# Group 4's second layer by seven products, three load buffers, and what moves with them

## The chip, the cores and the metric

The kernel runs on one core of a Trainium2 chip. The core has five engines that run their own instruction streams in order: TensorE (PE in the profile, its weight loads PEld), VectorE (DVE), ScalarE (ACT), GpSimd (POOL) and SyncE (SP), which here issues nearly all DMAs. The metric is device time in microseconds, from a median of several executions; less is better.

## The reference

Inputs are q, k and v (8 batches, 8 heads, 576 rows, 64 columns), a layer-norm gain of 512, and two weights of 512 x 2048 and 2048 x 512, all float32. Per head, attention goes by 32 landmarks (means of 18 rows each):

```python
A  = sm(q, k_lm)                 # 576 x 32
Bm = sm(q_lm, k_lm)              # 32 x 32
C  = sm(q_lm, k)                 # 32 x 576
Z  = Bm.T / (norm1(Bm) * norminf(Bm) + 1e-6)
for _ in range(6):
    Z = 2 * Z - Z @ Bm @ Z
x = A @ Z @ C @ v                # heads side by side: 8 x 576 x 512
```

Then a two-layer network with a residual: `x + relu(layer_norm(x) * g @ w1) @ w2`. The output is 8 x 576 x 512 float32.

## The kernel before, in words

**Attention** runs over sets of batches: 0, 1, 2, (3, 4), (5, 6) and 7. For each set, `Coming` holds the parts to come: q, k and v are loaded by SyncE into tiles of 576 KB (`stage`, six buffers), cast to fp16 by GpSimd, turned and summed to landmarks by VectorE, and the landmark sums of a pair are spread by a product `psl` (`spread`). `attention2` then computes scores (`psb`, `psec`, `psea`), the product with v (`pscv`), six iterations (`psn` on TensorE, `st` on VectorE in turn) and finally the rows: each row step is a pair of products `psy`, and VectorE divides into `xblk`, one tile of 128 rows by 512. 4608 rows make 36 blocks, four blocks a group: nine groups, 0 to 8. A group's blocks may come from two batches: batches 3 and 4 end in the middle of block 22, batches 5 and 6 in the middle of block 31.

**The network** is the generator `mlp`, which yields after every one or two matrix products. For each group it takes the normalized and transposed rows `xnT`, computes 16 tiles of the first layer (`psh`, four 128x512 products each, ScalarE's relu writes `hT`), then the second layer. `xnT` comes from four `xn` (one per block, on GpSimd for groups 2 and up) by four DMA transposes on SyncE; the first `psh` of a group waits for all four. `hT` has one buffer.

**Two forms of the second layer.** For groups below `G_FAST` (L45) each block is 16 products of 128x512 into `pso`, and VectorE makes the output tile `ot` from `pso`, the block's deviation factor and `xblk`. Those groups are centered only; the factor `rstd` is applied at the end. From `G_FAST` on, `second_layer` (L870) computes the 512 x 512 result as a 2 x 2 block product with seven half-size products, 16 products of 128x256 each (`psp1`, `psp6`, `psp5` ...), on sums of blocks: `w2_mix` t1 to t4 of the weight (made once, GpSimd) and s1 to s4 of `hT` (made per group, VectorE). Results are added into `xblk`, which is then stored. These groups need `xn` with the factor already in it, so `normalize` (L773) has to run ahead of `center`.

**The order of the work** is written out by hand. Each engine keeps program order. Between the steps of `attention2`, `fill(count)` takes `count` yields out of `mlp`; `steps` (L1150) lists, per set, the count and whether a cast and a turn job of the next set follow. `a_square` runs one waiting statistic per step, `settle` the delayed ones. `block_done` (L746) decides by group what a finished block causes. `center_in_turn` delays a block that is more than one group ahead of `mlp`. `prepare` casts, then issues loads until three are under way.

**Accumulators.** One bank `ps1` (tag `p1`: `psb`, `psse`, `psn`, and batch 7's `psl`), two score tiles of two banks `ps2` (tag `p2`: `psec`, `pscv`, `psea`, `pszc`, `psy`), and three banks `psM` (tag `pm`: `psh`, `pso`, `psp`, earlier `psl`).

In the changed stretch the set (5, 6) goes through its iterations (168 to 185 us) beside group 4's first layer, and through its rows (187 to 206 us) beside group 4's second layer; group 5 follows, beside batch 7.

Of the kernel before, what the change touches and what calls it, by code (L numbers as in the profile page):

```python
# [16 lines left out]
P = 128  # L17
# [3 lines left out]
def kernel(  # L21
# [20 lines left out]
    MCH = HID // P  # L42
    U = H // 4
    NJ = 9
    G_FAST = 5  # L45
    HK, HN = MCH // 2, DM // 2

    scale_qk = 1.0 / (D ** 0.5)
# [30 lines left out]
        keep(nc.tensor.matmul(o, i_, idn, is_transpose=True, tile_position=(0, 0)))  # L79


    def load(src, b, u, queue):
        t = stage.tile([P, 2, NJ, D], FP32, name="stg", tag="stg")
        keep(queue.dma_start(
            out=t[:],
            in_=src[b, 4 * u:4 * u + 4].rearrange("(r e) (t j) d -> (e t) r j d", e=2, j=NJ)))
        return t
# [11 lines left out]

    def load_turned(src, b, u, queue):
        t = stage.tile([P, 2, NJ, D], FP32, name="stg", tag="stg")
        rows = src[b, 4 * u:4 * u + 4].rearrange("(r e) (t j) d -> e t r j d", e=2, j=NJ)
        for half in range(2):
            keep(queue.dma_start(out=t[ts(half, 64), :, :, :], in_=rows[1 - half]))
        return t
# [399 lines left out]

    class Coming:  # L510
        def __init__(self, bs, first_by_pool=0):
            self.bs, self.first_by_pool = bs, first_by_pool
# [29 lines left out]
        def load(self, i, queue=nc.sync):  # L542
            nm, w = self.parts[i]
            b, u = self.units[w]
            src = {"q": q, "k": k, "v": v}[nm]
            self.stg[i] = (load_turned if nm == "v" and u % 2 == 1 else load)(src, b, u, queue)


        def cast(self, i):
# [50 lines left out]

        def spread(self, y):
            part = self.part.pop(y)
            late = self.bs[0] >= 7
            psl = (ps1 if late else psM).tile([P, 2, 8, LM], FP32, name="psl",
                                              tag="p1" if late else "pm")
            for half in range(2):
                MM(psl[:, half, :, :].rearrange("p k c -> p (k c)"),
                   spread16[:, half, :, :, :].rearrange("p e a w -> p (e a w)"),
                   part[:].rearrange("p n w r l x -> p (n w r l x)"))
            lm = asm.tile([P, 8, 2, LM], FP16, name="lm", tag="lm", bufs=3)  # L610
            scalar.copy(lm[:].rearrange("p k h c -> p h k c"), psl[:])
            for i, nm in enumerate(("q", "k")):
                for x in range(2):
                    self.lm[nm, 2 * y + x] = lm[:, ds(4 * i + 2 * x, 2), :, :].rearrange(
                        "p r h (l x) -> p r (h l) x", x=2)
# [130 lines left out]
    def block_done(j):  # L746
        g, u = divmod(j, 4)
        if g >= G_FAST:
            mean_of(j, dve)
            squares.append((at[0] + -4, lambda: normalize(j)))  # L750
            return
# [21 lines left out]
    def normalize(j):  # L773
        g, u = divmod(j, 4)
        square(j)
        if u == 0:
            lnvs[g] = mstat.tile([P, 4], FP32, name="lnv", tag="lnv")
            rstds[g] = mstat.tile([P, 4], FP32, name="rstd", tag="rstd")
        act(lnvs[g][:, u:u + 1], variances[g][:, u:u + 1], AF.Ln, bias=eps_ln[:],
            scale=1.0 / DM)  # L780
        act(rstds[g][:, u:u + 1], lnvs[g][:, u:u + 1], AF.Exp, scale=-0.5)
        center_in_turn(j)
# [72 lines left out]
    w21, w22 = w2_16[:, HK:MCH, 0:HN], w2_16[:, HK:MCH, HN:DM]  # L855

    def mixes_of_w2():
        for i in range(4):
            w2_mix.append(stage.tile([P, HK, HN], FP16, name=f"w2mix{i}", tag="stg"))
        for i in range(2):  # L860
            h_mix.append(stage.tile([P, HK, HN], FP16, name=f"hmix{i}", tag="stg"))
        t1, t2, t3, t4 = [t[:] for t in w2_mix]
        for o, a, b, op in ((t1, w12, w11, ALU.subtract), (t3, w22, w12, ALU.subtract),
                            (t2, t3, w11, ALU.add), (t4, w21, t2, ALU.subtract)):
            for k in range(0, HK, 2):
                pool.tensor_tensor(out=o[:, k:k + 2, :], in0=a[:, k:k + 2, :],
                                   in1=b[:, k:k + 2, :], op=op)
                yield

    def second_layer(g, hT, mixed):  # L870
        t1, t2, t3, t4 = [t[:] for t in w2_mix]
        h11, h12 = hT[:, 0:HK, 0:256], hT[:, HK:MCH, 0:256]
        h21, h22 = hT[:, 0:HK, 256:], hT[:, HK:MCH, 256:]
        s1, s2, s3, s4 = mixed
        x = [x_blk.pop(4 * g + u) for u in range(4)]

        def bank(name):
            return psM.tile([P, 2, HN], FP32, name=name, tag="pm")

        last = g == NGRP - 1  # L880

        def product(to, left, right, first=True, by_k=False):
            order = [(i, k) for i in range(2) for k in range(HK)]
            if by_k:
                order = [(i, k) for k in range(HK) for i in range(2)]
            for n, (i, k) in enumerate(order):
                apart = isinstance(to, list)
                MM(to[i][:] if apart else to[:, i, :], left[:, k, ts(i, P)], right[:, k, :],
                   start=first and (n == 0 or apart and k == 0), stop=k == HK - 1, skip=True)
                if n % 2 == 1 and n < 15:  # L890
                    yield True

        def add(engine, half, col, t, us=(0, 1)):
            for i in us:
                o = x[2 * half + i][:, ts(col, HN)]
                engine.tensor_tensor(out=o, in0=t[i][:] if isinstance(t, list) else t[:, i, :],
                                     in1=o, op=ALU.add)

        pa = bank("psp1")
        yield from product(pa, h11, w11)  # L900
        p1 = mout.tile([P, 2, HN], FP32, name="p1", tag="ot")
        scalar.copy(p1[:], pa[:])
        for half, col in ((0, 1), (1, 1), (1, 0)):
            add(pool, half, col, p1)
        yield True
        pb = bank("psp6")
        yield from product(pb, s2, t2, by_k=True)
        add(dve, 0, 1, pb)
        yield True
        yield from product(pa, h12, w21, False)  # L910
        add(dve, 0, 0, pa)
        if last:
            for u in (0, 1):
                store(4 * g + u, x[u], ts(0, HN))
        for k in range(0, HK, 4):
            dve.tensor_tensor(out=s4[:, k:k + 4, :], in0=h12[:, k:k + 4, :],
                              in1=s2[:, k:k + 4, :], op=ALU.subtract)
        yield True
        yield from product(pb, s3, t3, False)
        add(dve, 1, 1, pb)  # L920
        yield True
        pc = ([psM.tile([P, HN], FP32, name="psp5", tag="pm"),
               ps1.tile([P, HN], FP32, name="psp5", tag="p1")] if last else bank("psp5"))
        yield from product(pc, s1, t1)
        add(dve, 1, 1, pc)
        yield True
        yield from product(pb, h22, t4, False)
        add(dve, 1, 0, pb)
        for u in (2, 3):
            store(4 * g + u, x[u], ts(0, DM), last)  # L930
        yield True
        c = product(pc, s4, w22, False)
        for _ in range(4 if last else 7):
            next(c)
            yield True
        if last:
            add(dve, 0, 1, pc, (0,))
            store(4 * g, x[0], ts(1, HN), True)
        for _ in c:
            yield True  # L940
        add(dve, 0, 1, pc, (1,) if last else (0, 1))
        for u in (1,) if last else (0, 1):
            store(4 * g + u, x[u], ts(1, HN) if last else ts(0, DM), last)
        yield True

    def mix_of_h(hT, mixed, m):
        s1, s2, s3, _ = mixed
        h11, h21, h22 = hT[:, 0:HK, 0:256], hT[:, 0:HK, 256:], hT[:, HK:MCH, 256:]
        k0, k1 = {11: (0, 4), 13: (4, 6), 14: (6, 7), 15: (7, 8)}[m]
        n = ds(k0, k1 - k0)  # L950
        dve.tensor_tensor(out=s1[:, n, :], in0=h21[:, n, :], in1=h22[:, n, :], op=ALU.add)
        dve.tensor_tensor(out=s2[:, n, :], in0=s1[:, n, :], in1=h11[:, n, :], op=ALU.subtract)
        if m == MCH - 1:
            for k in range(0, HK, 4):
                dve.tensor_tensor(out=s3[:, k:k + 4, :], in0=h11[:, k:k + 4, :],
                                  in1=h21[:, k:k + 4, :], op=ALU.subtract)

    def mlp():
        for g in range(NGRP):
# [18 lines left out]
            else:  # L978
# [11 lines left out]
                for m in range(MCH):  # L990
# [6 lines left out]
                    act(hT[:, m, :], psh[:], AF.Relu)  # L997
                    if g >= G_FAST:
                        if m == 0:
                            while not h_mix:  # L1000
                                yield False
                            mixed = [h[:] for h in h_mix] + [hT[:, 0:HK, 256:],
                                                             hT[:, HK:MCH, 0:256]]
                        if m - 1 in (11, 13):
                            mix_of_h(hT, mixed, m - 1)
                        elif m == MCH - 1:
# [142 lines left out]

    steps = [[(10, 1, 0), (12, 1, 1)] + 6 * [(6, 1, 1)] + [(8, 1, 1)] + 5 * [(6, 0, 0)]]  # L1150
    steps += [[(6, 1, 0), (8, 1, 0), (12, 1, 0), (12, 1, 0), (6, 1, 0), (6, 1, 0)] + 4 * [(5, 1, 0)] + [(8, 0, 0)] + 3 * [(6, 0, 0)] + 7 * [(7, 1, 1)]]
    steps += [[(12, 1, 0), (14, 1, 1), (16, 1, 1), (16, 1, 1)] + 6 * [(9, 1, 1)] + [(10, 1, 1)] + 10 * [(8, 1, 1)]]
    steps += [[(15, 0, 0), (18, 0, 0)] + 6 * [(12, 0, 0)] + [(12, 0, 0)] + 5 * [(12, 0, 0)]]
    mixing = mixes_of_w2()
    for c, after, plan in zip(sets, sets[1:] + [None], steps):
# [3 lines left out]
        for n, ((count, casts, jobs), _) in enumerate(zip(plan, attention2(c.bs, c))):  # L1159
# [4 lines left out]
            a_square()  # L1164
            if after:
                prepare(after, casts, jobs)
            if c in sets[2:] and not sets[-1].casts:
                for _ in range(1):
                    next(mixing, None)
    settle()  # L1170
# [36 lines left out]
```

## Time and profile before

| | |
|---|---|
| median of 6 executions | 320.16 us (316.34 to 321.72) |
| profiled execution | 318.57 us |
| its span, first to last instruction | 316.8 us |
| granted TensorE clock | 1.000 |
| busy: TensorE / VectorE / ScalarE / GpSimd | 304.3 / 181.6 / 160.9 / 161.2 us |
| stretch 168 to 186 us: TensorE / VectorE / GpSimd busy | 17.33 / 8.09 / 13.48 us |
| stretch 186 to 202 us: TensorE / VectorE / GpSimd busy | 16.00 / 10.72 / 11.22 us |
| stretch 219 to 233 us: TensorE / VectorE / GpSimd busy | 14.00 / 8.82 / 7.39 us |

The span runs from the first to the last instruction of the profiled execution, and that execution's own time is 1.8 us longer. Busy times of different engines overlap. The stretches are those of group 4's first layer, group 4's second layer (classical form) and group 5's second layer (seven products). Matrix products overlap in the pipeline, so a product's mean duration in a list is longer than the pace; the pace is a stretch's time divided by its products. Times inside a stretch are given in us from the start of the span.

### The profile page before, as it was taken

The page shows a single profiled execution, that of the slowest core. Times are in us where ns is not written, and L with a number is a line of the kernel's source. Part 1 is how long each engine was busy: PE and PEld are TensorE (multiplying, and loading weights), DVE is VectorE, ACT ScalarE, POOL GpSimd, SP SyncE. Part 2 cuts the span into 40 slices and gives each one's busy share as a digit, 9 for nine tenths or more (in the row PEclk, how much of TensorE's full clock was granted, in tenths as well). Part 3 has the DMA queues.
Part 4 walks back from the last instruction along what each step waited for, and adds up shares of the span by engine and source line. Part 5 has one row for each costly group of instructions (what it writes and reads, how often), then busy time and mean ns, then how long its engine had stood idle before and what let it go on. Part 6 is the DMA issues. An engine that isn't in the chain of part 4 may idle for free.

```text
span 316.8 us, 8388 instructions
## 1 busy us (share of the span) xinstructions
PE 304.3 (96%) x3424; PEld 173.9 (55%) x3424; DVE 181.6 (57%) x487; ACT 160.9 (51%) x329; POOL 161.2 (51%) x218
## 2 busy tenths in 40 slices
PE   8889999999997989999999999999999999999994
PEld 8558754443443534544454444445854784685583
DVE  3667239868793325899376337746634860561372
ACT  2476853479225861267536646776038706505600
POOL 4489878908997695583003939900900360040050
PEclk9999999999999999999999999999999999999999
DMA  7999999769999995580087004330054016005013
GB/s 276 391 386 384 385 388 267 252 150 366 212 246 193 381 266 129 98 251 19 6 226 167 0 2 95 70 71 0 3 118 83 0 35 151 18 0 132 2 25 110
DMA packets 38862, 50.35 MB, mean 159 GB/s; under 512 B 17572, under 2 KB 18088, under 8 KB 38824
## 3 DMA queue, kind: packets, MB, share of 16 engines
q1 hardware_dynamic: 38504, 49.43, 54.9%
q8 instruction: 27, 0.44, 0.6%
q10 hardware_dynamic: 320, 0.39, 0.4%
q14 instruction: 11, 0.09, 0.1%
HBM read 36.70 MB, written 9.44 MB: 146 GB/s over the span
## 4 chain that ended last, share of the span: by engine, by line
PE 83%; DVE 9%; DMA 4%; issue 1%; ACT 1%; POOL 1%; SPq 0%; DVEq 0%; POOLq 0%
PE psh L75 40%; PE psp L75 16%; PE pso L75 15%; PE psy L75 3%; DVE part L69 2%; DMA stg<-in_k_dram 2%; DVE xblk L69 2%; PE psn L75 2%; PE pscv L75 2%; DMA xnT<-xn 1%; DVE ot L69 1%; PE psec L75 1%; DVE xT L69 1%; POOL natv L69 1%; PE psea L75 1%
## 5 line engine op out<-in xcount | busy, mean ns | idle before, releaser
L75 PE MATMUL psh<-xnT,w 128*128 128x512 f16 (+1 forms) x640 | 135.3, 359 | 1.3 <-DMA xnT<-xn 1.3
L69 ACT ACTIVATE hT<-psh 128x512 f16<-128x512 f32 x144 | 84.2, 598 | 78.3 <-PE psh L75 77.8
L75 PEld LDWEIGHTS <-w 128*128 128x128 f16 x640 | 58.7, 98 | 58.3 <-issue 4.6
L75 PEld LDWEIGHTS <-hT 128*128 128x128 f16 x640 | 60.9, 98 | 35.2 <-issue 1.5
L75 PE MATMUL pso<-w,hT 128*128 128x512 f16 x320 | 76.6, 380 | 0.0
L69 POOL TENSOR_TENSOR xblk<-p,xblk 128x256 f32<-128x256 f32 x24 | 17.4, 762 | 62.4 <-ACT p L69 62.4
L69 POOL CAST nat<-stg 128x1152 f16<-128x1152 f32 x28 | 31.6, 1145 | 16.0 <-DMA stg<-in_q_dram 14.4
L69 ACT ACTIVATE junk<-xblk,negm 128x512 f16<-128x512 f32 x36 | 25.9, 719 | 21.4 <-POOL negm L69 13.8
L69 POOL TENSOR_SCALAR xn<-xblk,negm,rstd 128x512 f16<-128x512 f32 x16 | 13.5, 856 | 43.8 <-ACT rstd L69 34.6
L69 DVE SCALAR_TENSOR_TENSOR xblk<-psy,rcpd 128x512 f32<-128x512 f32 (+1 forms) x40 | 27.6, 691 | 1.8
L69 DVE SCALAR_TENSOR_TENSOR st<-st,psn 128x128 f16<-128x128 f16 (+2 forms) x36 | 11.4, 316 | 28.0 <-PE psn L75 28.0
L69 DVE TENSOR_TENSOR xblk<-psp,xblk 128x256 f32<-128x256 f32 x48 | 18.2, 418 | 16.1 <-PE psp L75 15.9
L75 PE MATMUL psp<-w,hT 128*128 128x256 f16 x192 | 23.4, 273 | 0.0
L69 POOL CAST natv<-stg 128x1152 f16<-128x1152 f32 x16 | 18.3, 1161 | 7.2 <-DMA stg<-in_v_dram 7.2
L69 DVE TENSOR_TENSOR hmix<-hT 128x256 f16<-128x256 f16 (+2 forms) x16 | 6.8, 424 | 25.6 <-ACT hT L69 25.5
L69 DVE STREAM_TRANSPOSE xT<-nat 128x576 uint32<-128x576 uint32 x24 | 18.5, 769 | 0.0
L69 DVE TENSOR_REDUCE part<-xT 128x32 f16<-128x576 f16 x26 | 18.3, 745 | 0.1
L69 DVE SCALAR_TENSOR_TENSOR ot<-pso,rstd,xblk 128x512 f32<-128x512 f32 x20 | 14.9, 747 | 5.1 <-PE pso L75 5.0
L69 DVE RECIPROCAL rcpd<-psy 128x8 f32<-128x8 f32 (+1 forms) x40 | 8.1, 203 | 16.3 <-PE psy L75 15.7
L75 PE MATMUL psy<-zcbd,ea 128*128 128x260 f16 (+1 forms) x80 | 15.6, 277 | 0.7 <-DVE zcbd L69 0.5
L75 PE MATMUL psp<-w2mix,hT 128*128 128x256 f16 x128 | 15.5, 273 | 0.0
L75 PE MATMUL psp<-w2mix,hmix 128*128 128x256 f16 x128 | 15.3, 273 | 0.0
(116 smaller groups left out, 328.6 us busy)
## 6 DMA issues: line engine op xcount, KB each, us to landing
stg<-in_q_dram SPq DMA_DIRECT2D x16, 576.0 KB, 7.9
stg<-in_k_dram SPq DMA_DIRECT2D x16, 576.0 KB, 7.1
wstg<-in_moe_w_ch_dram SPq DMA_DIRECT2D x16, 512.0 KB, 6.9
stg<-in_v_dram SPq DMA_DIRECT2D x10, 576.0 KB, 10.5
out_dram<-ot SPq DMA_DIRECT2D x40, 128.0 KB, 2.7
stg<-in_v_dram SPq DMA_DIRECT2D x12, 288.0 KB, 11.5
out_dram<-xblk SPq DMA_DIRECT2D x26, 128.0 KB, 2.3
xnT<-xn SPq DMA_TRANSPOSE x28, 2.5
```

Source lines behind the costliest of these rows:

```text
L69: return lambda *args, **kw: keep(getattr(self.engine, op)(*args, **kw))
L75: keep(nc.tensor.matmul(o, l, r, start=start, stop=stop, tile_position=(rb, cb), skip_group_check=(skip or cb != 0)))
```

## The change

`G_FAST` becomes 4, so group 4's second layer also goes by seven products. The mixes of `w2` are therefore needed earlier and beside live load buffers: `t1` is made in place in the weight (`last_mix_of_w2`, four VectorE sums under group 4's first layer), the other three take three of the six buffers of `stage`, and the loads of batches 5 to 7 go through a ring of three. Group 4 keeps `s1` in two output tiles and makes `s2` in place of `h11` after the first product (`mix_less`); its seven products stand in another order, and one of them takes the bank `ps1`. Groups 4, 5 to 8 are normalized four blocks at a time (`normalize`), and group 4's means go to GpSimd. The spreads of the sets from batch 5 on take a score tile (`ps2`) instead of `psM` or `ps1`. The counts of the set (5, 6) become 7 in the iterations (9 before) and 10 in the rows (8 before). The mixing starts in set (3, 4) at step 16.

```diff
-    G_FAST = 5
+    G_FAST = 4
...
+            t = None
+            if self.bs[0] >= 5:
+                if len(ring) < 3:
+                    ring.append(stage.tile([P, 2, NJ, D], FP32, name="ring", tag="stg"))
+                    ring_at[0] = len(ring) - 1
+                t = ring[ring_at[0]]
+                ring_at[0] = (ring_at[0] + 1) % 3
...
-            late = self.bs[0] >= 7
-            psl = (ps1 if late else psM).tile([P, 2, 8, LM], FP32, name="psl",
-                                              tag="p1" if late else "pm")
+            late = self.bs[0] >= 5
+            psl = (ps2 if late else psM).tile([P, 2, 8, LM], FP32, name="psl",
+                                              tag="p2" if late else "pm")
...
         if g >= G_FAST:
+            if g in (4,):
+                later.append(lambda: mean_of(j, pool))
+                squares.append((at[0], lambda: normalize(j)))
+                return
...
         square(j)
+        if g not in (3,):
+            if u == 3:
+                deviations(g)
+                for i in range(j - 3, j + 1):
+                    center_in_turn(i)
+            return
...
+    def last_mix_of_w2(k):
+        dve.tensor_tensor(out=w12[:, k:k + 2, :], in0=w12[:, k:k + 2, :],
+                           in1=w11[:, k:k + 2, :], op=ALU.subtract)
...
+        def mix_less(o, a):
+            n = HK // len(a)
+            for k in range(0, HK, 4):
+                dve.tensor_tensor(out=o[:, k:k + 4, :], in0=a[k // n][:, ds(k % n, 4), :],
+                                  in1=o[:, k:k + 4, :], op=ALU.subtract)
+
+        def mix(o, a, b):
+            for k in range(0, HK, 4):
+                dve.tensor_tensor(out=o[:, k:k + 4, :], in0=a[:, k:k + 4, :],
+                                  in1=b[:, k:k + 4, :], op=ALU.subtract)
+
+        def by_way_of_sbuf(bank_, name, where):
+            t = mout.tile([P, 2, HN], FP32, name=name, tag="ot")
+            scalar.copy(t[:], bank_[:])
+            for half, col in where:
+                add(pool, half, col, t)
+
+        def p1_done(pa):
+            by_way_of_sbuf(pa, "p1", ((0, 1), (1, 1), (1, 0)))
+
+        def p2_done(pa):
+            add(dve, 0, 0, pa)
...
+            mix(s4, h12, s2[0])
...
         pa = bank("psp1")
         yield from product(pa, h11, w11)
+        p1_done(pa)
+        if not apart:
+            mix_less(h11, s1)
...
+        pc = bank("psp5")
         yield from product(pc, s1, t1)
         add(dve, 1, 1, pc)
         yield True
+        yield from product(pa, h12, w21, False)
+        p2_done(pa)
+        yield True
+        pb = bank("psp6")
+        yield from product(pb, s2, t2)
+        add(dve, 0, 1, pb)
+        yield True
+        pd = (bank("psp4") if g in (3,) else
+              ps1.tile([P, 2, HN], FP32, name="psp4", tag="p1"))
+        yield from product(pd, h22, t4)
+        by_way_of_sbuf(pd, "p4", ((1, 0),))
+        yield True
+        yield from product(pc, s4, w22, False)
+        add(dve, 0, 1, pc)
+        for u in (0, 1):
+            store(4 * g + u, x[u], ts(0, DM))
+        yield True
+        yield from product(pb, s3, t3, False)
+        by_way_of_sbuf(pb, "p7", ((1, 0), (1, 1)))
...
+                                mixed = [[mout.tile([P, HK // 2, HN], FP16, name="s1", tag="ot")[:]
+                                          for _ in range(2)], []]
...
+                        if g == G_FAST and m in (2, 4, 6, 8):
+                            last_mix_of_w2(m - 2)
...
-    steps += [[(12, 1, 0), (14, 1, 1), (16, 1, 1), (16, 1, 1)] + 6 * [(9, 1, 1)] + [(10, 1, 1)] + 10 * [(8, 1, 1)]]
+    steps += [[(12, 1, 0), (14, 1, 1), (16, 1, 1), (16, 1, 1)] + 6 * [(7, 1, 1)] + [(10, 1, 1)] + 10 * [(10, 1, 1)]]
...
-            if c in sets[2:] and not sets[-1].casts:
+            if (c.bs[0], n) >= (3, 16):
```

## The prediction

> **What bounds the kernel now.** I read the busy shares first, then the slices, the chain that ended last, TensorE's waits, and then the stretches of the engines around the change.
>
> ```profile
> PE 304.3 (96%) x3424; PEld 173.9 (55%) x3424; DVE 181.6 (57%) x487; ACT 160.9 (51%) x329; POOL 161.2 (51%) x218
> ...
> PE   8889999999997989999999999999999999999994
> ...
> PEclk9999999999999999999999999999999999999999
> ```
>
> TensorE is busy in 96% of the span at a full clock; no other engine passes 57%. Only less TensorE work, or a new TensorE stall, moves the end. The chain in order of time gives the price of both forms of a layer, because the last groups run there undisturbed:
>
> ```profile
> 197.78 1.73 PE pso L75 x8
> ...
> 274.09 12.23 PE psp L75 x112
> 286.31 13.81 PE psh L75 x64
> 300.13 12.25 PE psp L75 x112
> ```
>
> A 128x512 product takes 13.81/64 = 0.216 us (so do the `pso` of group 4's second layer: 1.73/8), a 128x256 one of the seven-product form 12.25/112 = 0.109 us. TensorE's own waits add up to 7.6 us, most of them in the first 120 us; one lies in the changed stretch, at 180.56:
>
> ```profile
> PE psn L75 <- ACT lm L69: 0.7, 1, 0.7
> ```
>
> There an iteration product `psn` waited until ScalarE had emptied the spread `psl`, which stood in the same single bank.
>
> **What the change takes away.** (a) Group 4's second layer: 64 x 0.216 = 13.8 us becomes 112 x 0.109 = 12.25 us: -1.56 us, between -1.5 and -1.6 by the rows. (b) Batch 7's spread goes to a score bank, so the 0.7 us above ends: -0.7 (0 if VectorE is late there anyway). Nothing else on TensorE goes: its order keeps all other products. So -2.26 us is the most there is, 0.7% of the time.
>
> **What it adds, edit by edit.**
>
> Three load buffers: a load is now issued only when the cast three loads earlier is done. The loads of batches 5 to 7 used to be issued in a bunch (six within 100.25 to 104.2). Now the load that takes the buffer of the cast of 105.23 goes out when that cast ends, at 106.4, and with 4.9 us to land (issue 100.25, cast released at 105.2) it is there at 111.3; the one after the cast that ends at 110.5 at 115.4. GpSimd wants them at 111.56 and 115.72 (its casts of before). Margins of 0.3 to 0.5 us, and behind them GpSimd idles 3.25 us before 125.39: cost 0, at most some 1 to 3 us if loads come later and that cover is used up. Behind a waiting load on SyncE's queue stand only further loads and stores there.
>
> The mixes of w2: GpSimd makes twelve pieces of 1.15 us in place of sixteen, between 135 and 181 instead of 178 to 206, beside its casts. First used at about 191: cost 0 on TensorE. Their four missing pieces become four VectorE sums in `w12`, 0.42 us each by the 128x512 `hmix` rows.
>
> Centering by groups of four: group 4's four `xn` can start only after its deviations (ScalarE, about 157.2 in place of 136.5). The first is done at 158.0, the fourth transpose goes out 3.9 us later and lands 2.5 us after that (rows under (d)): 164.4; the first layer begins at 168.07, slack 3.6 us. Behind them on GpSimd stand batch 7's casts (160.3 instead of 139.2); VectorE's transpose of the first (160.58) starts 0.8 us late, and `psn` uses that stretch at 169.7. Group 7: after the row that completes block 31 TensorE has 28 x 0.216 + 112 x 0.109 + 8 x 0.11 = 19 us of work, the chain to its input takes about 12. Cost 0; 1 to 2 us if such slack is used up.
>
> Spreads in the score bank: two buffers, last read over 1 us before each spread: 0. Rows further apart: the same row products; cost 0 as long as VectorE keeps up.
>
> (c) **VectorE in the iterations.** Between 168 and 182 the steps have 7 products in place of 9, and VectorE gets the four sums in `w12`. In VectorE's sums of two SBUF operands a wait shows. First GpSimd's timeline, then VectorE's at the same time (start, us, engine, operation, out<-in):
>
> ```profile
> 139.15 3.32 POOL L69 CAST nat<-stg 128x1152 f16<-128x1152 f32 x3
> ```
> ```profile
> 140.18 1.24 DVE L69 TENSOR_TENSOR part<-sT 128x64 f16<-128x64 f16 x1
> ...
> 143.37 0.39 DVE L69 TENSOR_TENSOR part<-sT 128x64 f16<-128x64 f16 x1
> ```
>
> The same operation takes 1.24 or 0.39 us: it ends when GpSimd's current instruction ends (the second cast, at 141.4). GpSimd will be busy without a break from 157 to 181, so each of the five such sums ahead of the fifth iteration may wait up to 1.15 us. Laid out with rows (0.42 + two reduces of 0.66 + 0.35 in one step; 0.42 + 0.70 + 0.20 + 0.25 in the next two) VectorE is 1.2 us ahead of `psn` without waits and up to 3.7 us behind with all of them. The eleven rows of `part<-sT` have a mean of 0.49 against 0.19 alone, a wait of 0.3: five of them less the lead of 1.2 give 0.3. As GpSimd never pauses here I take +0.5 us; bounds 0 and 3.7.
>
> (d) **Group 5's input.** This is the term that I expect to matter. Before, groups 5 and later were centered block by block. Now block 23 completes under group 4's first product, the four `xn` stand on GpSimd behind six `xblk` additions of that product, and group 5 begins as soon as the seventh product ends. Rows for each link:
>
> ```profile
> 221.65 4.18 POOL L69 TENSOR_TENSOR xblk<-p,xblk 128x256 f32<-128x256 f32 x6 [15.19 <-ACT p L69]
> 225.82 3.22 POOL L69 TENSOR_SCALAR xn<-xblk,negm,rstd 128x512 f16<-128x512 f32 x3
> ```
> ```profile
> 220.13 1.29 DVE L69 TENSOR_TENSOR hT<-hT 128x1024 f16<-128x1024 f16 x2
> ...
> 225.49 1.49 DVE L69 TENSOR_TENSOR hT<-hT,hmix 128x1024 f16<-128x1024 f16 x2
> ```
> ```profile
> 220.98 0.58 ACT L69 COPY p<-psp 128x512 f32<-128x512 f32 x1 [1.42 <-PE psp L75]
> ```
> ```profile
> 264.14 5.16 SPq L807 DMA_TRANSPOSE xnT<-xn  x4
> ```
> ```profile
> xnT<-xn SPq DMA_TRANSPOSE x28, 2.5
> ```
>
> From the end of the first product: copy 0.7 (product end to GpSimd's start), six additions 4.2, one `xn` 0.77, last of four transposes issued 3.9 later (5.16 less one issue of 1.2), 2.5 to land, 0.1: 12.15 us. TensorE has meanwhile six products and five row pairs: 96 x 0.109 + 5 x 0.225 = 11.6 us (0.225: what a `psy` pair takes between products at 195.45). So 0.5 us is missing even undisturbed. And the three `xn` above took 3.22 us where 3 x 0.75 = 2.25 is usual: they stood behind VectorE's pair of `hT` sums at 225.49. Group 4's form has two such pairs (`mix_less`, and the fourth mix), both inside this chain: 12.15 + 2 x 0.95 - 11.6 = +2.4 us. Bounds: 0.5 without any meeting, 3.6 if each pair also waits for half an addition. Behind the stall on TensorE stands everything.
>
> The Trainium skill, page "SBUF — State Buffer", section "Who interferes with whom", says that a VectorE instruction with two SBUF inputs and a GpSimd instruction that reads SBUF exclude each other for a whole instruction, whichever started first. The 1.24 us and the 3.22 us rows agree with it. By that rule both pairs of (d) count and the sum stays at +0.6; without any exclusion (d) would be 0.5 us, (c) 0, and the sum -1.8 us. The page "TensorE: Matmul & The Clock Gate", section "HAM oscillation — how this bites in real kernels", speaks against the change: gaps over about 3.4 us halve the clock for a while, so a stall of (d)'s upper bound could cost some 1.7 us more by that page; no gap here is longer than 1.3 us, and the clock row shows no drop.
>
> **Sum.** -1.56 - 0.7 + 0.5 + 2.4 = +0.6 us. The profiled execution took 318.57 us, its span 316.8 us; the span would become 317.4, that execution 319.2. The six runs have their median at 320.16, 1.6 us above the profiled one; on that scale the forecast is 320.8 us. About 1% (3.2 us) is what a measurement of this kernel can tell from no change, so this is none.
>
> **Rivals.**
> 1. The stalls do not come: the pairs miss GpSimd's work, or a late VectorE delays the second layer so that the input is there in time. Then -2.26 + 0.5, 318.4 us. For it: (d) undisturbed misses by 0.5 us only. Against: the pair at 225.49 met GpSimd exactly so.
> 2. Slower: two-input sums on VectorE behind GpSimd's instructions, in both places. It has some 16 us of work in the 17 us from the last iteration to the end of group 4's second layer (zcbd 1.35, sums for the mixes 5.5, six rows at 1.1, additions 2.7), so the waits have no room. Price: (c) at 3.7 and (d) at 3.6: -2.26 + 7.3 = +5.0, 325.2 us. It decides from 5.5 us of stalls on, where the loss passes 1%. For it: GpSimd has no gap from 157 to 181. Against: `part<-sT` waits 0.3 us on the mean, far less than a whole instruction.
> 3. Three buffers starve the casts: 1 to 3 us more than the forecast, 322 us. Against: the margins above and the idle 3.25 us.
>
> **Chances.** Forecast 0.5 (its own range 318.8 to 322.8), rival 1 0.2, rival 2 0.25, rival 3 0.05. Faster by over 1% would need 316.9, under the most that TensorE can give: 0.04 for what I overlook. Slower by over 1%, from 323.4 on: rival 2 and a little of the forecast's tail, 0.28. Within 1%: 0.68. The range goes from rival 1 less 0.8 to rival 2: 317.6 to 325.2.
>
> **What would show it.** (a) 112 `psp` in group 4, 0.109 us each. (b) No `psn` waiting for `lm`. (c) `psn` or `psl` waiting for VectorE's `st` or `part` between 173 and 182. (d) `psh` waiting about 2.4 us for a transpose near 199 us, the largest wait of the second half. Buffers: no new GpSimd wait for a load. The forecast is wrong if that `psh` wait is absent, or if TensorE waits for VectorE inside group 4's products.

## The result, and the profile after

The median is 321.25 us for the changed kernel (34 executions, 318.67 to 325.86) and 319.25 us for the kernel before on the same chips (71 executions). The ratio is 1.0077, with a 95% interval of 1.0059 to 1.0096: about 2.5 us slower (1.9 to 3.1). The ratio leaves out executions over 1.5% above the fastest of their kernel, so it is more than the 2.0 us between the two medians. The profiled execution of the changed kernel took 319.92 us and its span is 318.2 us, 1.35 us more than the profiled one of before. By the prediction's bound of 1% this is no change, as forecast (+0.6 us, 320.8 us). But the interval does not reach zero, so it is a small loss, and a part of it comes from places that the prediction had priced at nothing.

The page of the changed kernel: busy time and share of each engine, then TensorE's busy tenths and granted clock in 40 slices of 8 us.

```profile
PE 302.4 (95%) x3472; PEld 177.2 (56%) x3472; DVE 193.0 (61%) x505; ACT 157.8 (50%) x308; POOL 167.6 (53%) x226
...
PE   7889999999998999999999998799999799999994
...
PEclk9999999999999999999999999999999999999999
```

TensorE works 1.9 us less than before (302.4 against 304.3), and two holes have come into the row of slices, at about 200 and 250 us. TensorE's waits name them (waited for: us in total, times, longest):

```profile
PE psh L75 <- DMA xnT<-xn: 3.8, 2, 3.2
PE psp L75 <- DVE xblk L69: 1.6, 1, 1.6
```

The wait of `psn` for `lm` (0.7 us before) is no longer in the list. The chain in order of time goes through each hole. First group 5's input, then group 6's second layer; at the end a seven-product layer that runs undisturbed (start, us, what):

```profile
186.12 0.59 ACT p L69
...
186.79 1.77 POOL xblk L69 x2
...
189.75 2.13 POOL xblk L69 x3
191.88 3.62 POOL xn L69 x4
...
198.38 2.40 DMA xnT<-xn
...
249.34 4.46 POOL xblk L69 x5
253.83 0.42 DVE xblk L69
...
254.30 7.24 PE psp L75 x64
...
275.35 12.23 PE psp L75 x112
```

**The first hole, 3.23 us at 200.9.** GpSimd's timeline (start, us, engine, operation, out<-in), then VectorE's and SyncE's in the same stretch:

```profile
186.79 5.09 POOL L69 TENSOR_TENSOR xblk<-p,xblk 128x256 f32<-128x256 f32 x6 [7.29 <-ACT p L69]
191.84 3.99 POOL L69 TENSOR_SCALAR xn<-xblk,negm,rstd 128x512 f16<-128x512 f32 x4
```
```profile
186.94 2.27 DVE L69 TENSOR_TENSOR hT<-s,hT 128x1024 f16<-128x1024 f16 x2
...
191.53 1.50 DVE L69 TENSOR_TENSOR hT<-hT 128x1024 f16<-128x1024 f16 x2
```
```profile
193.62 5.95 SPq L827 DMA_TRANSPOSE xnT<-xn  x4
```

The six additions stand ahead of group 5's four `xn`. VectorE's first pair of sums meets the additions (5.09 us instead of 4.2), its second pair meets the first `xn` (four in 3.99 us instead of 3.0). Then the four transposes take 5.95 us to issue where 5.16 is usual.

**The second hole, 1.65 us at 254.3.** GpSimd's and VectorE's timelines around group 6's second layer:

```profile
244.98 3.85 POOL L69 TENSOR_SCALAR xn<-xblk,negm,rstd 128x512 f16<-128x512 f32 x4 [20.59 <-ACT rstd L69]
249.33 5.15 POOL L69 TENSOR_TENSOR xblk<-p,xblk 128x256 f32<-128x256 f32 x6 [0.50 <-DVE hmix L69]
```
```profile
250.16 2.36 DVE L69 TENSOR_TENSOR hT<-hT 128x1024 f16<-128x1024 f16 x2
...
253.49 0.76 DVE L69 TENSOR_TENSOR xblk<-psp,xblk 128x256 f32<-128x256 f32 x2
```

The same pair of sums in the kernel before:

```profile
249.57 1.28 DVE L69 TENSOR_TENSOR hT<-hT 128x1024 f16<-128x1024 f16 x2
```

Group 7's four `xn` now come in one row and meet VectorE's sums for group 6. VectorE runs late, so its last pair of sums (2.36 us, 1.28 before) meets the six additions, and its addition of the bank `psp6` ends at 254.25. The fourth product accumulates into that bank; TensorE could have begun it at 252.65.

**The sum from the two traces.** -1.56 (products, at the pace of the undisturbed layers), -0.67 (`lm`), +3.23, +1.65: +2.65 us. One more difference, of -1.33 us at 117 us, turns up below; with it the sum is +1.32, and the two profiled executions differ by 1.35. That these two agree so closely is partly luck. Waits for `xnT` near 97 us are left out of the sum: they are 0 to 2.3 us long in different executions, in kernels with and without the change, and were 0.6 us here against 1.3 before. Other short waits in the first 100 us are left out too.

### The profile page after: what moved, and what is told of

It reads as the page before. It is cut to its first block, busy times and chain, and to the rows that moved or that the text cites. A ratio compares the mean times of both kernels' runs of the same rounds, so it can differ in the third digit from the quotient of the medians.

```text
span 318.2 us, 8507 instructions
## 1 busy us (share of the span) xinstructions
PE 302.4 (95%) x3472; PEld 177.2 (56%) x3472; DVE 193.0 (61%) x505; ACT 157.8 (50%) x308; POOL 167.6 (53%) x226
## 4 chain that ended last, share of the span: by engine, by line
PE 67%; DVE 10%; DMA 10%; POOL 7%; issue 2%; SPq 2%; ACT 1%; POOLq 0%; DVEq 0%
PE psh L75 34%; PE psp L75 15%; PE pso L75 9%; DMA stg<-in_v_dram 4%; POOL xblk L69 3%; DVE xblk L69 3%; DMA stg<-in_k_dram 2%; DMA xnT<-xn 2%; DVE part L69 2%; PE psn L75 2%; DMA stg<-in_q_dram 2%; PE pscv L75 2%; PE psy L75 1%; POOL xn L69 1%; DVE ot L69 1%
## 5 line engine op out<-in xcount | busy, mean ns | idle before, releaser
L75 PEld LDWEIGHTS <-hT 128*128 128x128 f16 x672 | 64.4, 98 | 32.1 <-issue 2.9
L75 PE MATMUL pso<-w,hT 128*128 128x512 f16 x256 | 61.3, 380 | 0.0
L69 POOL TENSOR_TENSOR xblk<-p,xblk 128x256 f32<-128x256 f32 x36 | 27.0, 785 | 64.7 <-ACT p L69 48.7
L69 POOL TENSOR_SCALAR xn<-xblk,negm,rstd 128x512 f16<-128x512 f32 x20 | 17.1, 865 | 39.3 <-ACT rstd L69 39.3
L69 DVE TENSOR_TENSOR xblk<-psp,xblk 128x256 f32<-128x256 f32 x56 | 21.2, 418 | 15.3 <-PE psp L75 15.2
L75 PE MATMUL psp<-w,hT 128*128 128x256 f16 x240 | 29.3, 273 | 0.0
L69 POOL CAST nat<-stg 128x1152 f16<-128x1152 f32 x16 | 18.1, 1146 | 12.2 <-DMA stg<-in_q_dram 10.6
L75 PE MATMUL psp<-w2mix,hT 128*128 128x256 f16 x176 | 21.5, 273 | 1.6 <-DVE xblk L69 1.6
L69 POOL CAST nat<-ring 128x1152 f16<-128x1152 f32 x12 | 13.5, 1146 | 4.3 <-DMA ring<-in_q_dram 4.3
L69 POOL CAST natv<-stg 128x1152 f16<-128x1152 f32 x10 | 11.4, 1162 | 7.1 <-DMA stg<-in_v_dram 7.0
```

The costliest lines, as they stand in the source:

```text
L69: return lambda *args, **kw: keep(getattr(self.engine, op)(*args, **kw))
L75: keep(nc.tensor.matmul(o, l, r, start=start, stop=stop, tile_position=(rb, cb), skip_group_check=(skip or cb != 0)))
```

## The experiments

All are compared with the kernel before on the same chip. "Waits from 140 us on" are TensorE's gaps of over 0.1 us in the profiled execution, from one product to the next.

**1. Block by block again for groups 5 to 8.**

```diff
-        if g not in (3,):
+        if g in (4,):
             if u == 3:
                 deviations(g)
```

> Groups 5 to 8 are normalized and centered block by block again, as in the kernel before; only group 4 keeps the grouping by four, and all other parts of the change stay. Theory (the loss is two stalls of TensorE, 3.23 us ahead of group 5's first layer and 1.65 us in group 6's second layer, both because four xn come at once on GpSimd): both go, so 4.9 us less than the changed kernel, 2.2 to 2.6 us less than the kernel before, a ratio of about 0.9925. Rival (group 4's seven products with their additions and sums load VectorE and GpSimd so that TensorE waits there in any case): the stall at group 5 shrinks by at most the one xn that moves, 1 us or so, and the time stays within 1 us of the changed kernel, ratio 1.005 to 1.008.

Measured: 315.44 us, ratio 0.9928 (0.9896 to 0.9961). Waits from 140 us on: 0.28 us for `xnT` at 197.3, and 0.11 and 0.45 us for `xblk` in group 6. As the theory has it. The 0.28 us are what the last `xn`, which still stands behind the six additions, costs; the 0.45 us come from VectorE's other pair of sums in group 6 (0.70 + 1.18 us), beside four `xn` of group 8.

**2 and 3. The two stalls apart.**

```diff
-        if g not in (3,):
+        if g not in (5,):
```

The second of the two has `(7,)` there.

> Only group 5 is normalized block by block; groups 6 to 8 stay by four. Theory: three of group 5's four xn and transposes are done before the six additions, so the first-layer stall at 200.9 us goes (3.23 us less) and the one in group 6 stays: 0.6 to 0.8 us less than the kernel before, ratio 0.9975. Rival (the seven products themselves): no more than 1 us less than the changed kernel, ratio 1.005 or more.

> Only group 7 is normalized block by block. Theory: group 7's xn leave the stretch in which VectorE makes group 6's sums, so psp no longer waits 1.65 us for the VectorE addition near 254 us, and the 3.2 us ahead of group 5 stay: 1.65 us less than the changed kernel, 0.8 us more than the kernel before, ratio 1.0025. Rival (this stall is a chance of the one profiled execution, or comes from the other edits): the time of the changed kernel, ratio 1.0077.

Measured: 317.03 us and 0.9971 (0.9935 to 1.0007) with group 5 block by block, 319.98 us and 1.0029 (0.9991 to 1.0067) with group 7 block by block. In the first, `psh` waits 0.34 us and `psp` still 1.64; in the second, whose profiled execution had a mean granted clock of 0.989, `psh` waits 2.87 us and `psp` 0.12. Each edit takes away its own stall and leaves the other one, so the two are independent. Group 4's seven products don't need the first stall: in experiment 2 they are there without it.

**4. The six additions behind the four xn.**

```diff
-        p1_done(pa)
-        if not apart:
+        if apart:
+            p1_done(pa)
+        else:
+            p1 = mout.tile([P, 2, HN], FP32, name="p1", tag="ot")
+            scalar.copy(p1[:], pa[:])
             mix_less(h11, s1)
...
         yield from product(pa, h12, w21, False)
         p2_done(pa)
+        for half, col in ((0, 1), (1, 1), (1, 0)):
+            add(pool, half, col, p1)
```

> The change with one move: group 4's six GpSimd additions of the first product are emitted behind group 5's four xn (after the third product) instead of ahead of them; ScalarE's copy and all else stay. Theory (the xn and their transposes are late only because they queue behind the six additions): deviations are ready at 188.5 us, four xn take 3 to 4 us, the last transpose lands near 197, no stall at group 5: 3.2 us less than the changed kernel, 0.6 to 0.8 us less than the kernel before, ratio 0.9975. Rival (SyncE's transposes or ScalarE's deviations are the limit): the stall keeps at least 2 us, ratio 1.004 or more. What could spoil it: VectorE's addition of the fourth product has to wait for the first two of the late additions, up to 1 us, with rows behind it.

Measured: 316.48 us, ratio 0.9954 (0.9913 to 0.9995). GpSimd's timeline and SyncE's:

```profile
188.69 3.96 POOL L69 TENSOR_SCALAR xn<-xblk,negm,rstd 128x512 f16<-128x512 f32 x4 [9.11 <-ACT rstd L69]
192.62 5.57 POOL L69 TENSOR_TENSOR xblk<-p,xblk 128x256 f32<-128x256 f32 x8
```
```profile
189.48 5.14 SPq L827 DMA_TRANSPOSE xnT<-xn  x4
```

The first `xn` waits for the deviations alone, 188.69 instead of 191.84, and the transposes are all issued at 194.6. No `psh` waits. So the first stall is a matter of the order on GpSimd's queue: neither the deviations nor the transposes are too slow. The 1.65 us in group 6 are still there.

**5. Both repairs.**

> Centering block by block for groups 5 to 8, and the six additions behind block 23's xn: the two repairs together. Theory: what is left ahead of group 5 after the first repair alone (0.28 us) goes too, the 0.45 us in group 6 that VectorE's last pair of sums leaves there stays: 2.6 to 2.9 us less than the kernel before, ratio 0.992. Rival (the late additions delay VectorE's and ScalarE's work behind them): the gain is under 2 us, ratio 0.994 or more.

The edits of the first and the fourth experiment together:

```diff
-        if g not in (3,):
+        if g in (4,):
...
-        p1_done(pa)
-        if not apart:
+        if apart:
+            p1_done(pa)
+        else:
+            p1 = mout.tile([P, 2, HN], FP32, name="p1", tag="ot")
+            scalar.copy(p1[:], pa[:])
...
+        for half, col in ((0, 1), (1, 1), (1, 0)):
+            add(pool, half, col, p1)
```

Measured: 315.2 us, ratio 0.9905 (0.9863 to 0.9947). No wait for `xnT`; 0.12 and 0.45 us in group 6.

**6. The rest of the change without its point.**

```diff
-    G_FAST = 4
+    G_FAST = 5
```

> The whole change except its seven products in group 4 (the switch point stays at group 5): group 4's second layer by 64 products of 128x512, no sums of hT and no additions of products there, its xn centered only. Theory: 1.56 us more products, no stall ahead of group 5 because nothing stands before its xn on GpSimd, the 1.65 us in group 6 stay, the 0.67 us at the spread of the kernel before are gone: 0.9 to 1.1 us more than the kernel before, ratio 1.003. Rival (the ring, the earlier mixes or the wider rows cost something by themselves): 2 us or more above the kernel before, ratio 1.006 or more.

Measured: 317.46 us, ratio 0.9984 (0.9949 to 1.0019). The only wait from 140 us on is 1.40 us for `xblk` in group 6. The stalls are as expected, but the time is about 1.5 us better than the theory gives: the rest of the change seems to have a gain in it that I hadn't seen. A candidate is found below.

**7. Centering by four alone.**

```diff
         square(j)
+        if g not in (3,):
+            if u == 3:
+                deviations(g)
+                for i in range(j - 3, j + 1):
+                    center_in_turn(i)
+            return
         if u == 0:
```

> The kernel before with one edit: groups 5 to 8 are normalized and centered four blocks at a time. Theory (the four xn of group 7 fall into VectorE's sums of group 6, and the emptier ScalarE copies the first product earlier): TensorE waits 1.6 us for VectorE's addition of the third or fourth product of group 6 and nowhere else: 1.6 us more than the kernel before, ratio 1.005. Rival (the stall needs the rest of the change): no difference, ratio 1.000.

Measured: 318.28 us, ratio 0.9966 (0.9921 to 1.0011), and no stall in group 6. The theory fell in this form: four `xn` at once aren't enough. Its timelines show why, GpSimd and then VectorE:

```profile
239.01 3.03 POOL L69 TENSOR_SCALAR xn<-xblk,negm,rstd 128x512 f16<-128x512 f32 x4 [16.33 <-ACT rstd L69]
247.25 4.17 POOL L69 TENSOR_TENSOR xblk<-p,xblk 128x256 f32<-128x256 f32 x6 [5.21 <-ACT p L69]
```
```profile
241.67 0.90 DVE L69 TENSOR_TENSOR hmix<-hT 128x1024 f16<-128x1024 f16 x1 [0.46 <-ACT hT L69]
...
246.10 1.29 DVE L69 TENSOR_TENSOR hT<-hT 128x1024 f16<-128x1024 f16 x2
```

The four `xn` are nearly over (242.0) when VectorE begins its sums, and the pair of sums is over when the additions begin. In the changed kernel the rows of batch 7 that complete group 7 stand later against the network. Group 4's second layer now yields 56 times instead of 64, so the network is 8 yields further on. The new counts take 6 x 7 + 10 + 10 x 10 = 152 yields instead of 6 x 9 + 10 + 10 x 8 = 144, which is another 8. Together they make 16 yields, 3.5 us at 0.216. Experiment 6 has only the 8 yields of the counts, and its stall is 1.40 us.

**8. The price of the meetings.**

```diff
-            mix(s4, h12, s2[0])
+            if apart:
+                mix(s4, h12, s2[0])
...
-        if not apart:
-            mix_less(h11, s1)
```

> The change without the four sums of 128x1024 that VectorE makes for group 4 during and after its first products (mix_less and the fourth mix are left out, so that group 4's rows are computed from unmixed halves); products, additions and xn stay. It prices the meetings of these sums with GpSimd. Theory: the six additions take 4.2 us instead of 5.05 and the first xn 0.76 instead of 1.75, so the wait of psh ahead of group 5 falls from 3.23 to 1.3 to 1.5 us. Rival (no exclusion, GpSimd is only slow there): the wait stays at 2.8 us or more.

Measured in one execution (320.32 us): `psh` waits 1.35 us instead of 3.23. GpSimd's timeline:

```profile
189.30 4.17 POOL L69 TENSOR_TENSOR xblk<-p,xblk 128x256 f32<-128x256 f32 x6 [7.29 <-ACT p L69]
193.47 3.02 POOL L69 TENSOR_SCALAR xn<-xblk,negm,rstd 128x512 f16<-128x512 f32 x4
```

Without VectorE's four sums the additions are back at 4.17 us and the `xn` at 3.02. The sums cost (5.09 - 4.17) + (3.99 - 3.02) = 1.89 us, which is all of the difference. The transposes took 5.95 us here too.

**9 to 11. The second condition.** One kernel has the rows put back by 16 yields, one has this and the late additions, and one has the kernel before with both conditions and nothing else of the change.

```diff
-    steps += [[(15, 0, 0), (18, 0, 0)] + 6 * [(12, 0, 0)] + [(12, 0, 0)] + 5 * [(12, 0, 0)]]
+    steps += [[(15, 0, 0), (18, 0, 0)] + 6 * [(10, 0, 0)] + [(8, 0, 0)] + 5 * [(12, 0, 0)]]
```

The third has `6 * [(14, 0, 0)] + [(16, 0, 0)]` there.

> The change, with 16 yields of the network fewer ahead of batch 7's rows (its six iterations get 10 in place of 12, the step before its rows 8 in place of 12). The run with centering by four alone had no stall in group 6, so that edit isn't enough by itself. New theory: the stall needs two things together, four xn at once and batch 7's rows standing 16 yields (two row steps) later against the network than before, because group 4 yields 8 times less by products of the new form and the list of counts takes 8 more; then group 7's last deviations and its xn fall into group 6's sums. With the rows put back it goes though the xn still come by four: group 6 without a stall, group 5's 3.2 us unchanged, 0.6 to 1.0 us above the kernel before, ratio 1.003. Rival (something else of the change, the ring, the mixes or the second spread, makes VectorE late there): the stall stays at 1.4 us or more, ratio 1.0077.

> The same, with group 4's six additions behind group 5's xn as well: both stalls are addressed by moving work only, centering stays by four. Theory: no wait of TensorE over 0.2 us from 140 us on, 2.2 to 2.9 us less than the kernel before, ratio 0.991 to 0.993, the same as with block-by-block centering and late additions. Rival (the shorter iterations of batch 7 make TensorE wait for VectorE or ScalarE): some psn or psy waits, gain under 1.5 us, ratio 0.995 or more.

> The kernel before with centering by four for groups 5 to 8 (the run that showed no stall) and batch 7's rows 16 yields later (iterations 14 in place of 12, the step before the rows 16 in place of 12): the two conditions together and nothing else of the change. Theory: the stall of group 6 appears, 1.3 to 1.7 us ahead of its fourth product behind VectorE's addition; 1.5 us more than the kernel before, ratio 1.005. Rival (it needs another part of the change): no wait over 0.2 us there, ratio 0.998 to 1.000.

Measured with the rows put back: 319.19 us, ratio 1.0017 (0.9988 to 1.0046). The `xn` are over before the sums, as in experiment 7, and the pair of sums is undisturbed:

```profile
243.00 3.03 POOL L69 TENSOR_SCALAR xn<-xblk,negm,rstd 128x512 f16<-128x512 f32 x4 [17.14 <-ACT rstd L69]
251.24 4.18 POOL L69 TENSOR_TENSOR xblk<-p,xblk 128x256 f32<-128x256 f32 x6 [5.21 <-ACT p L69]
```
```profile
250.10 1.28 DVE L69 TENSOR_TENSOR hT<-hT 128x1024 f16<-128x1024 f16 x2
```

No `psp` waits; `psh` waits 3.58 us ahead of group 5. With the late additions as well: 314.81 us (six executions), ratio 0.9879 (0.9837 to 0.9921), and TensorE has no wait of over 0.1 us from 140 us on. The gain is 1.0 us above the upper end of the theory, which did not have the 1.33 us at 117 us: -1.56 - 0.67 - 1.33 = -3.56 us. This is the best version of the case, 3.9 us (2.5 to 5.2) faster than the kernel before, and it is the change with work moved and nothing taken back.

With both conditions in the kernel before: 321.78 us (six executions), ratio 1.0112 (1.0066 to 1.0157). The stall is there in its old size, 1.6 us ahead of the fourth product, and GpSimd's timeline is that of the changed kernel, 0.56 us later:

```profile
PE psp L75 <- DVE xblk L69: 1.6, 1, 1.6
```
```profile
245.54 3.85 POOL L69 TENSOR_SCALAR xn<-xblk,negm,rstd 128x512 f16<-128x512 f32 x4 [19.73 <-ACT rstd L69]
249.88 5.16 POOL L69 TENSOR_TENSOR xblk<-p,xblk 128x256 f32<-128x256 f32 x6 [0.50 <-DVE hmix L69]
```

So these two conditions together are enough for the stall, with nothing else of the change. Centering by four alone gives none (experiment 7), and neither does the whole change with the rows put back. The later rows were not run alone: in the changed kernel they leave 0.45 us with centering block by block (experiment 1) and 0.12 us with only group 7 block by block (experiment 3). The time rose by 3.6 us (2.1 to 5.0), 2 us more than the stall; its profile has no other new wait from 140 us on, and where the rest comes from stays open.

**12. The spread alone.**

```diff
-            psl = (ps1 if late else psM).tile([P, 2, 8, LM], FP32, name="psl",
-                                              tag="p1" if late else "pm")
+            psl = (ps2 if late else psM).tile([P, 2, 8, LM], FP32, name="psl",
+                                              tag="p2" if late else "pm")
```

> The kernel before with one edit: batch 7's spread takes a score tile instead of the single bank. Theory: the wait of psn for ScalarE's copy of the spread at 180.6 us goes and none takes its place: 0.7 us less, ratio 0.998. Rival (VectorE's st or the score tiles are late there anyway): another wait of 0.3 us or more in the iterations, ratio 0.999 to 1.001.

Measured: 318.25 us, ratio 0.999 (0.9956 to 1.0024). The wait for `lm` is gone and no wait of over 0.14 us is left from 140 us on. The time can't tell 0.7 us from nothing.

## Why the prediction was right or wrong

**(a) Products: right.** A seven-product layer takes 12.23 us for 112 products. Group 4's takes 13.73 us (183.95 to 197.68) with six row pairs in it; less 6 x 0.22 that is 12.4 us, 0.2 us above the price.

**(b) The spread: right.** The 0.67 us went, alone (experiment 12) and in the change, and nothing took its place.

**Three buffers: no starving, but not nothing.** GpSimd has no new wait for a load that reaches TensorE. What I priced at "cost 0, at most some 1 to 3 us" seems to have brought a gain instead. In the four kernels with the old loads (before, and experiments 7, 11, 12) TensorE stands still for 0.6 to 2.0 us in the middle of a `psn`, between 114 and 118 us, for nothing that the profile names ("issue"). TensorE's timeline of the kernel before:

```profile
116.07 0.23 PE L75 MATMUL psn<-st 32*32 32x64 f16 x5
117.63 0.26 PE L75 MATMUL psn<-st 32*32 32x64 f16 x11 [1.33 <-issue]
```

In the ten kernels with the ring (after, and 1 to 6 and 8 to 10) that wait is 0.12 us or less. With the old loads the DMA engines are full from 105 to 120 us without a break; in the changed kernel they fall to a share of 0.26 between 110 and 112. That would account for the better time of experiment 6: 1.40 - 0.67 - 1.33 = -0.6 us, and -0.5 (-1.6 to +0.6) was measured.

The traces narrow down what TensorE waits for. In all four kernels it stops at the same place, between the fifth and the sixth `psn` of one group. The DMA listing of every run has a queue marked `instruction` (q8) with 27 transfers of 16 KB, most likely TensorE's own program: it runs some 6900 products and weight loads, VectorE as the next only some 500 instructions. In the kernel before and experiments 7, 11 and 12 one of these transfers ends at 115.9, 112.9, 116.1 and 115.6 us, and TensorE goes on 1.4 to 1.8 us later each time. This transfer starts 6.2 to 7.7 us after the one before it; in the ten kernels with the ring it is 3.3 to 5.4 us. So a part of the program that came late behind the bunch of loads fits all four standstills. That is argued and not shown: the ring was not run alone, and the ten kernels have other parts of the change too.

**(c) Iterations: 0.5 us forecast, 0 measured, with almost nothing to spare.** The meetings came. VectorE's timeline in the changed kernel, the four sums in `w12` and one of the two in `part`, then the `psn` that follows on TensorE:

```profile
168.55 1.02 DVE L69 TENSOR_TENSOR w<-w 128x512 f16<-128x512 f16 x1
...
171.14 0.53 DVE L69 TENSOR_TENSOR w<-w 128x512 f16<-128x512 f16 x1
...
172.52 1.13 DVE L69 TENSOR_TENSOR part<-sT 128x64 f16<-128x64 f16 x1
...
173.90 1.07 DVE L69 TENSOR_TENSOR w<-w 128x512 f16<-128x512 f16 x1
...
175.96 0.41 DVE L69 SCALAR_TENSOR_TENSOR st<-st,psn 128x256 f16<-128x256 f16 x1
176.78 0.42 DVE L69 SCALAR_TENSOR_TENSOR st<-st,psn 128x256 f16<-128x256 f16 x1 [0.42 <-PE psn L75]
177.12 1.36 DVE L69 TENSOR_TENSOR w<-w 128x512 f16<-128x512 f16 x1
```
```profile
176.42 0.30 PE L75 MATMUL psn<-st 32*32 32x64 f16 x16
```

Over 0.42 us and 0.19 us alone these are 3.2 us of waits. The part that failed is "VectorE is 1.2 us ahead of `psn` without waits": 2.3 us of them lie ahead of the `st` at 175.96, which ends at 176.37, and the `psn` that needs it begins at 176.42. So the lead was about 2.3 us, and the measured 0 is partly luck: 0.05 us were left. All the meetings in full, the prediction's upper bound, would have been 1.2 + 3.7 = 4.9 us; about half of that came in time to matter. With this, rival 2 (meetings in both places, from 5.5 us of stalls on) was out: the meetings came in both, but in the iterations they were covered.

**(d) Group 5's input: right in mechanism and place, 3.23 us instead of 2.4.** The two meetings cost 1.89 us (experiment 8) against the 2 x 0.95 of the prediction. The term that was too small is the transposes: four issues in 5.95 us instead of 5.16, one of them 2.0 us. In the profiles in which the four `xn` come at once, the four transposes take either 5.12 to 5.24 or 5.6 to 6.3 us; the row that I had taken is of the first kind.

**"Centering by groups of four ... Cost 0" and "Rows further apart: the same row products; cost 0 as long as VectorE keeps up": the steps that failed.** For group 7 I had only asked whether its input comes in time for `psh`, and it did. I hadn't asked whom the four `xn` meet on the way there, and I had priced the counts by their products alone, not by what stands beside what 50 us later. Together they cost 1.65 us; the first alone cost no stall, and of the second without the first at most 0.45 us were seen. The prediction's own test, "TensorE waits for VectorE inside group 4's products", looked one layer too early.

**The rule of the skill.** The Trainium skill, page "SBUF — State Buffer", section "Who interferes with whom", was to make both pairs of (d) count. Experiment 8 agrees with that, with 0.92 and 0.97 us.

**The sum.** The terms gave +0.6 us where the traces give +1.3 for the two profiled executions. That these lie so close is luck in part: two terms that the prediction did not have, +1.65 in group 6 and -1.33 at 117 us, nearly cancel, and so do 0 instead of +0.5 in (c) and 0.8 more in (d). So is the nearness of 320.8 to 321.25 us: the forecast stood on a median of 320.16 us for the kernel before, which is 319.25 in 71 executions. The comparison's +2.5 us is larger than +1.3, and lower granted clocks can account for a part of the difference, as the last section shows.

## What to carry to other kernels

A step that is moved has to be checked against every engine's timeline where it lands, not only against the deadline of its own result: here four `xn` were in time for their reader and still made another group's sums, additions and products late. In a schedule that is written out in counts, count the yields: a layer that yields 8 times less and a list that takes 8 more shift everything behind them, and a collision that four `xn` at once don't make alone appears 50 us later. Before an edit with a small sure gain is given up, look for the queue order that causes its stall: moving six additions and two counts turned +0.8% into -1.2%.

## What the runs showed of the hardware

**A short standstill can cost the clock, and not in every execution.** In the profiled execution of the changed kernel the clock stayed at 1.00 through the 3.23 us hole. With the rows put back (experiment 9) the hole was 3.58 us, and in the stretches after it the clock fell. The columns are stretch, its length, then busy us and instructions of TensorE, weight loads, VectorE, ScalarE and GpSimd, then the granted clock, DMA share and GB/s:

```profile
199.00:201.00 2.00, 0.29 (x2) 0.21 (x3) 0.00 (x0) 0.00 (x0) 2.00 (x4) 1.00 0.48 101
201.00:203.00 2.00, 2.00 (x9) 0.76 (x8) 0.00 (x0) 0.60 (x1) 2.00 (x4) 0.72 0.81 192
203.00:205.00 2.00, 2.00 (x7) 0.86 (x6) 0.91 (x3) 1.30 (x3) 1.13 (x2) 0.50 0.87 201
205.00:207.00 2.00, 2.00 (x11) 1.00 (x10) 0.15 (x1) 1.33 (x3) 0.00 (x0) 0.92 0.76 166
```

That is 2 x (0.28 + 0.50 + 0.08) = 1.72 us lost. The same happened behind a hole of only 1.98 us, the "issue" wait in experiment 12:

```profile
114.00:116.00 2.00, 1.10 (x10) 0.32 (x8) 0.24 (x1) 0.60 (x1) 1.84 (x4) 1.00 1.01 242
116.00:118.00 2.00, 0.93 (x13) 0.42 (x14) 0.42 (x1) 0.08 (x1) 1.84 (x3) 0.80 1.06 225
118.00:120.00 2.00, 2.00 (x21) 0.67 (x20) 0.03 (x1) 0.89 (x2) 1.92 (x4) 0.50 1.05 167
120.00:122.00 2.00, 2.00 (x23) 0.72 (x22) 0.65 (x2) 0.22 (x1) 1.10 (x1) 0.84 0.89 209
```

Again 2 x (0.20 + 0.50 + 0.16) = 1.72 us. In experiment 3 the 2.87 us hole ahead of group 5 was followed by 0.87, 0.50 and 0.78 in three such stretches from 204 us on, 1.70 us lost. Near 97 us, the kernel before had holes of 0.56 and 1.28 us and no drop, and experiment 2 had holes of 0.67 and 1.21 us and a drop to 0.92, 0.50 and 0.73. So the length of one hole doesn't decide it: 3.23 us passed, 1.98 and 1.21 us did not. The Trainium skill, page "TensorE: Matmul & The Clock Gate", section "HAM oscillation — how this bites in real kernels", puts the limit at gaps of about 3.4 us, and the throttled time in its example at about 1.67 us, half of which is lost. Here the limit doesn't hold in experiment 12, and the throttled time is twice as long: 1.72 us lost are 3.44 us at half speed. The prediction had set aside "some 1.7 us" for a stall of (d)'s upper bound only. The size fits the measured 1.72 us, although half of the example's 1.67 us would be 0.8.

**It shows in the median.** Of 32 executions of the changed kernel that the comparison used, the 6 with a mean clock of 1.000 took 319.6 us on average and the 11 with 0.995 took 321.3: 1.7 us more, one such loss. 14 executions of the kernel before, from the experiments, with a clock of 1.000 took 318.3 us on average. At a full clock the change thus costs about 1.3 us, which is what the traces sum up to; at 0.995 it is 2.0 us (11 against 9 executions), so this split is an estimate. The mean clock is 0.9938 in the changed kernel's 32 and 0.9966 in 67 of the kernel before, and 0.0028 x 318 us = 0.9 us. Together this is 2.2 us of the 2.5 measured. That the changed kernel's extra losses follow the hole at 200 us is likely from experiments 3 and 9, where two of the three profiled executions with that hole in nearly its full length have a drop behind it. But only profiled executions show where a loss lies, so it is argued and not shown.
